# TensorE in program order, attention and M in tiles of two banks, weights converted by bits with seven blocks in flight, batch 0's second product by rows of w_out

## The chip, the cores and the metric

The kernel runs on one core of a Trainium2 chip. The metric is the device time of one execution in microseconds (us), the median of several runs. The engines are named as in the profile: PE is TensorE (PEld its weight loads), DVE is VectorE, ACT is ScalarE, POOL is GpSimd, SP is SyncE. SBUF is the memory on the core that all engines work in, PSUM the accumulators that PE writes; a bank of PSUM holds 512 fp32 values on each of 128 partitions, and there are eight.

## The reference

Per batch b (8 of them) and head h (8), x is 512 x 64 and state 32 x 64. Tokens read the states, states read the tokens, and the rows of both go through a feed-forward block with an ELU between its two products.

```python
scores  = x @ state.T / sqrt(64)          # 512 x 32
xread   = softmax(scores,  -1) @ state    # 512 x 64
scores2 = state @ x.T / sqrt(64)          # 32 x 512, the same numbers transposed
sread   = softmax(scores2, -1) @ x        # 32 x 64
rows    = concat([xread, sread])          # per batch 544 rows, heads side by side: 512 wide
h   = rows @ w_in                         # 4352 x 512 @ 512 x 2048
g   = where(h > 0, h, exp(min(h, 0)) - 1)
out = g @ w_out                           # 4352 x 2048 @ 2048 x 512
```

x and state are fp32, w_in and w_out arrive as 64-bit floats, and the output is fp32.

## The kernel before

**Setup.** The states are loaded with 32 small DMAs, half of them issued by SP and half by POOL, and turned by PE into kT (line 114). x of a batch, 1 MB, is loaded in four DMAs, two issued by SP and two by POOL (line 93); batches 0 and 1 at once, batch b+2 behind batch b+1's attention.

**Weights** (load_weights, lines 117 to 153). Both matrices come in 32 blocks of 128 x 512 64-bit values, 512 KB each: 16 of w_in (c is one of four groups of 512 columns, n one of four groups of 128 rows), 16 of w_out (fo is a group of 128 rows). A block is loaded into a "raw" tile (three tiles, which also held the states) by SP, and seven DVE steps over 128 x 512 elements make fp32 from the two 32-bit words of each value: exponent out, limited, moved, sign put in (lines 126 to 139), mantissa words joined and scaled (144 to 151). Every step that reads words of the raw tile reads every second word.

**Attention of a batch** (attention, lines 266 to 276), in steps: four times turn_x (four transposes on PE into one bank, a copy by ACT, line 168), scores (by_state, line 177: eight products of 64 x 32 weights, on parts of the array), two softmaxes (heads' halves g = 0, 1; lines 196 to 225) on DVE, ACT and POOL, one along the free dimension for the states (result a_s) and one in 32 x 32 blocks for the tokens (result t), turn_tokens (DVE transpose, aT), turn_state (four transposes of a_s on PE, copy by ACT to aT_s), state_read (16 products, line 246, result into xT_state for all batches), and the load of a later x.

**M.** xread @ w_in is not formed by way of xread. make_m (line 264) multiplies kT with 512 columns of w_in, by by_state in the same way as the scores, to M of 2 x 128 x 512; then h = aT @ M (ffn1, line 293) takes two products of 128 x 512 for each of the 16 groups fo of hidden columns.

**Feed-forward.** elu (lines 282 to 285): exp on ACT, min on DVE, then (e - 1) max h on DVE into g[fo]. ffn2 (line 318) sums 16 products over fo for each of four chunks c of 128 tokens, one PSUM bank (o_ps) for each; ACT or DVE copies it out (line 325), SP stores two chunks together (line 353). After the eight batches the 256 state rows go through the same block (lines 306, 318, 368).

**PSUM.** Eight banks: three one-bank tiles for everything in attention and M (ps_a), three for h, two for o.

**Order.** The text is written in program order: batch 0's attention with a load of w_in between its steps, the rest of w_in, M for the first columns; then per batch 16 times ffn1, with M for the next columns behind fo = 1, 5 and 9, a block of w_out (batch 0 only) and a step of the next batch's attention; then four chunks of ffn2, with M for the next batch behind chunk 2. A planner, which runs when the kernel is built, fixes the order of instructions on each engine before the run. It takes what is written first when its inputs are ready by its own estimate of times, on PE as on the other engines. Each engine then works through its own list in order, and DMAs issued by one engine are issued in that engine's order.

Of the kernel before, what the change touches and what calls it, by code (L numbers as in the profile page):

```python
# [15 lines left out]
PSUM = bass.MemoryType.PSUM  # L16


@with_exitstack
def kernel(  # L20
# [11 lines left out]
    nc = tc.nc  # L32
# [23 lines left out]
    cpool = ctx.enter_context(tc.tile_pool(name="const", bufs=1))  # L56
    xpool = ctx.enter_context(tc.tile_pool(name="x", bufs=2))
    apool = ctx.enter_context(tc.tile_pool(name="attn", bufs=2))
    xtpool = ctx.enter_context(tc.tile_pool(name="xT", bufs=4))
    atpool = ctx.enter_context(tc.tile_pool(name="aT", bufs=4))  # L60
    atspool = ctx.enter_context(tc.tile_pool(name="aT_s", bufs=1))
    mpool = ctx.enter_context(tc.tile_pool(name="m", bufs=2))
    rawpool = ctx.enter_context(tc.tile_pool(name="raw", bufs=3))
    wpool = ctx.enter_context(tc.tile_pool(name="pow", bufs=2))
    small = ctx.enter_context(tc.tile_pool(name="small", bufs=4))
    gpool = ctx.enter_context(tc.tile_pool(name="g", bufs=FO + 1))
    epool = ctx.enter_context(tc.tile_pool(name="elu", bufs=4))
    opool = ctx.enter_context(tc.tile_pool(name="o", bufs=2))
    ps_a = ctx.enter_context(tc.tile_pool(name="ps_a", bufs=3, space=PSUM))
    ps_h = ctx.enter_context(tc.tile_pool(name="ps_h", bufs=3, space=PSUM))  # L70
    ps_o = ctx.enter_context(tc.tile_pool(name="ps_o", bufs=2, space=PSUM))

    def bank(shape, name):
        return ps_a.tile(shape, FP32, tag="a", name=name)

# [13 lines left out]
    def load_x(b):  # L89
        x_t[b] = xpool.tile([P, R, DM], FP32, name="x_sb")  # L90
        x_v = x[b].rearrange("h (p r) d -> p r h d", r=R)
        for r in range(R):
            (nc.sync, nc.gpsimd)[r % 2].dma_start(
                out=x_t[b][:, r].rearrange("p (h d) -> p h d", d=D), in_=x_v[:, r]
            )

    def setup():
        make_identity(nc, ident)
        s_v = state.rearrange("(q b) (m c) n d -> q m b n c d", q=2, c=2)
        raw = [rawpool.tile([P, NP, P], FP32, tag="raw", name="s_sb") for q in range(2)]  # L100
        for q in range(2):
            for m in range(NP):
                for b in range(B // 2):
                    (nc.sync, nc.gpsimd)[q].dma_start(  # L104
                        out=raw[q][b * NS : (b + 1) * NS, m].rearrange("p (c d) -> p c d", c=2),
                        in_=s_v[q, m, b],
                    )
        for b in range(2):
            load_x(b)
        for q in range(2):  # L110
            ps = bank([P, NP, P], "k_ps")
            for m in range(NP):
                nc.tensor.transpose(ps[:, m], raw[q][:, m], ident)
            nc.vector.tensor_copy(out=kT[:, :, q * P : (q + 1) * P], in_=ps)

    def load_weights(dst, src):


        raw = rawpool.tile([P, 512], moe_w_in.dtype, name="raw")
        k = src.shape[-1]  # L120
        nc.sync.dma_start(out=raw.rearrange("p (j k) -> p j k", k=k), in_=src)
        words = raw.bitcast(U32).rearrange("p (j k w) -> p j k w", k=k, w=2)
        lo, hi = words[:, :, :, 0], words[:, :, :, 1]
        power = wpool.tile([P, 512], U32, name="power").rearrange("p (j k) -> p j k", k=k)

        nc.vector.tensor_scalar(  # L126
            out=power, in0=hi, scalar1=20, scalar2=0x7FF,
            op0=ALU.logical_shift_right, op1=ALU.bitwise_and,
        )
        low = 1023 - 127  # L130
        nc.vector.tensor_scalar(  # L131
            out=power, in0=power, scalar1=float(low), scalar2=float(low + 255),
            op0=ALU.max, op1=ALU.min,
        )
        nc.vector.tensor_scalar(  # L135
            out=power, in0=power, scalar1=float(-low), scalar2=float(1 << 23),
            op0=ALU.add, op1=ALU.mult,
        )
        nc.vector.scalar_tensor_tensor(  # L139
            out=power, in0=hi, scalar=0x80000000, in1=power,  # L140
            op0=ALU.bitwise_and, op1=ALU.bitwise_or,
        )

        nc.vector.tensor_scalar(  # L144
            out=hi, in0=hi, scalar1=0xFFFFF, scalar2=0x100000,
            op0=ALU.bitwise_and, op1=ALU.bitwise_or,
        )
        nc.vector.scalar_tensor_tensor(  # L148
            out=dst, in0=lo, scalar=2.0**-32, in1=hi, op0=ALU.mult, op1=ALU.add
        )  # L150
        nc.vector.scalar_tensor_tensor(  # L151
            out=dst, in0=dst, scalar=2.0**-20, in1=power.bitcast(FP32),
            op0=ALU.mult, op1=ALU.mult,
        )
    def load_w_in(c, n):
        cols = slice(c * 512, (c + 1) * 512)
        load_weights(w_in[:, n : n + 1, cols], w_in_v[:, n : n + 1, cols])

    def load_w_out(fo):
        load_weights(w_out[:, fo : fo + 1], w_out_v[:, fo : fo + 1])  # L160

    def turn_x(b, m):

        ps = bank([P, R, P], "xT_ps")
        for r in range(R):
            nc.tensor.transpose(ps[:, r], x_t[b][:, r, m * P : (m + 1) * P], ident)  # L166
        st[b, m] = xtpool.tile([P, R * P], FP32, name="xT")
        nc.scalar.copy(out=st[b, m], in_=ps.rearrange("p r q -> p (r q)"))  # L168

    def by_state(b, name, rhs):  # L170


        ps = [bank([P, 512], name) for g in range(G)]
        for m in range(NP):
            for g in range(G):
                d = slice(g * D, (g + 1) * D)
                nc.tensor.matmul(  # L177
                    ps[g][m * NS : (m + 1) * NS],
# [8 lines left out]
    def scores(b):  # L187

        for g, ps in enumerate(by_state(b, "s_ps", [st[b, m] for m in range(NP)])):
            softmaxes(b, g, ps)  # L190
# [41 lines left out]
    def turn_state(b, g):  # L232
        ps = bank([P, R, P], "sT_ps")
        a = st[b, g, "a_s"].rearrange("p (r q) -> p r q", r=R)
        for r in range(R):
            nc.tensor.transpose(ps[:, r], a[:, r], ident)  # L236
        if g == 0:
            st[b, "aT_s"] = atspool.tile([P, R, G, P], FP32, name="aT_s")
        nc.scalar.copy(out=st[b, "aT_s"][:, :, g], in_=ps)  # L239

    def state_read(b):

        ps = bank([P, NP, G, NS], "sr_ps")
        for m in range(NP):
            for r in range(R):
                nc.tensor.matmul(  # L246
                    ps[:, m],
                    x_t[b][:, r, m * P : (m + 1) * P],
                    st[b, "aT_s"][:, r, :, m * NS : (m + 1) * NS],
# [9 lines left out]
    def make_m(b, c):  # L259
# [3 lines left out]
        for g, ps in enumerate(by_state(b, "m_ps", [w_in[:, m, cols] for m in range(NP)])):  # L263
            (nc.scalar.copy, nc.vector.tensor_copy)[g % 2](out=m_t[b, c][:, g], in_=ps)  # L264

    def attention(b):
        steps = []
        steps += [lambda m=m: turn_x(b, m) for m in range(NP)]
# [132 lines left out]
```

## Time and profile before

| | us |
|---|---|
| median of 3 runs | 920.93 (920.3 to 921.58) |
| the profiled execution, its own time | 921.35 |
| the profiled execution, span of its trace | 919.6 |
| granted clock, mean over the span | 0.965 |

Busy time of each engine, and what the DMAs moved: PE 860.6 us, DVE 359.6, ACT 156.5, POOL 58.1; 35.07 MB. The span starts with the first instruction of the kernel; the profiled execution's own time has 1.75 us around it. In rows of a timeline the columns are start, length (both us), engine, line, operation, output and inputs, partitions x elements, and the count; matmul rows carry the size of the weights too. In rows of a view of stages they are the stage, its length, and busy time with the number of instructions for each engine, then the granted clock as a share, the DMAs' share and their rate.

### The profile page before, as it was taken

The page shows a single profiled execution, that of the slowest core. Times are in us where ns is not written, and L with a number is a line of the kernel's source. Part 1 is how long each engine was busy: PE and PEld are TensorE (multiplying, and loading weights), DVE is VectorE, ACT ScalarE, POOL GpSimd, SP SyncE. Part 2 cuts the span into 40 slices and gives each one's busy share as a digit, 9 for nine tenths or more (in the row PEclk, how much of TensorE's full clock was granted, in tenths as well). Part 3 has the DMA queues.
Part 4 walks back from the last instruction along what each step waited for, and adds up shares of the span by engine and source line. Part 5 has one row for each costly group of instructions (what it writes and reads, how often), then busy time and mean ns, then how long its engine had stood idle before and what let it go on. Part 6 is the DMA issues. An engine that isn't in the chain of part 4 may idle for free.

```text
span 919.6 us, 7252 instructions
## 1 busy us (share of the span) xinstructions
PE 860.6 (94%) x2824; PEld 392.7 (43%) x2824; DVE 359.6 (39%) x755; ACT 156.5 (17%) x290; POOL 58.1 (6%) x70
## 2 busy tenths in 40 slices
PE   4185889999999999999999999999999999999997
PEld 2141243445444444445444544454444444444773
DVE  1979999616102720183007500570027102600220
ACT  1111222113001310141004200330023101300110
POOL 5100020001000200010001100010001000000000
PEclk9565989999999999999999999999999999999999
DMA  7354333002000010002000200000000000000000
GB/s 178 96 160 143 131 100 131 23 24 47 0 24 23 16 32 23 24 1 46 24 0 24 47 0 24 23 1 1 23 24 1 0 23 24 1 0 24 23 1 23
DMA packets 27043, 35.07 MB, mean 38 GB/s; under 512 B 19329, under 2 KB 19585, under 8 KB 27009
## 3 DMA queue, kind: packets, MB, share of 16 engines
q1 hardware_dynamic: 25216, 30.15, 10.5%
q0 software_dynamic: 1792, 4.46, 2.1%
q8 instruction: 22, 0.36, 0.2%
q14 instruction: 13, 0.10, 0.0%
HBM read 25.69 MB, written 8.91 MB: 38 GB/s over the span
## 4 chain that ended last, share of the span: by engine, by line
PE 84%; DVE 9%; DMA 3%; ACT 1%; SPq 1%; issue 0%; POOL 0%; DVEq 0%; ACTq 0%; POOLq 0%
PE o_ps L318 50%; PE h_ps L293 22%; PE m_ps L177 4%; PE h_ps L306 3%; DMA raw<-in_moe_w_in_dram 3%; PE sr_ps L246 3%; PE xT_ps L166 1%; DVE power L139 1%; DVE w_in L148 1%; DVE power L131 1%; DVE power L126 1%; DVE g_sb L285 1%; SPq L104 1%; PE sT_ps L236 1%; DVE raw L144 1%; DVE power L135 1%
## 5 line engine op out<-in xcount | busy, mean ns | idle before, releaser
L318 PE MATMUL o_ps<-w_out,g_sb 128*128 128x512 f32 x1088 | 473.2, 593 | 1.7 <-DVE total L214 1.7
L318 PEld LDWEIGHTS o_ps<-w_out,g_sb 128*128 128x128 f32 x1088 | 205.5, 190 | 265.0 <-issue 257.2
L293 PE MATMUL h_ps<-aT,m_sb 128*128 128x512 f32 x512 | 244.4, 616 | 12.8 <-DVE g_sb L285 11.7
L293 PEld LDWEIGHTS h_ps<-aT,m_sb 128*128 128x128 f32 x512 | 94.3, 195 | 132.9 <-issue 89.6
L282 ACT ACTIVATE e_sb<-h_ps 128x512 f32<-128x512 f32 (+1 forms) x144 | 82.6, 573 | 329.1 <-PE h_ps L293 285.5
L325 DVE COPY o_sb<-o_ps 128x512 f32<-128x512 f32 x17 | 11.7, 691 | 324.0 <-PE o_ps L318 324.0
L283 DVE TENSOR_SCALAR e_sb<-e_sb 128x512 f32<-128x512 f32 (+1 forms) x144 | 63.9, 444 | 92.7 <-ACT e_sb L282 92.7
L285 DVE SCALAR_TENSOR_TENSOR g_sb<-e_sb,h_ps 128x512 f32<-128x512 f32 (+1 forms) x144 | 93.9, 652 | 12.0 <-PE o_ps L318 8.4
L325 ACT COPY o_sb<-o_ps 128x512 f32<-128x512 f32 x17 | 10.0, 586 | 304.8 <-PE o_ps L318 304.8
L177 PE MATMUL m_ps<-w_in,kT 64*32 64x512 f32 x512 | 54.4, 620 | 2.1 <-DVE w_in L151 1.0
L264 DVE COPY m_sb<-m_ps 128x512 f32<-128x512 f32 x32 | 21.8, 682 | 85.0 <-PE m_ps L177 84.9
L211 POOL TENSOR_TENSOR t_sb<-t_sb,top_t 128x512 f32<-128x512 f32 x16 | 17.4, 1088 | 575.7 <-DVE total L214 485.7
L246 PEld LDWEIGHTS sr_ps<-aT_s,x_sb 128*128 128x128 f32 x256 | 32.6, 209 | 7.7 <-ACT e_sb L282 5.0
L246 PE MATMUL sr_ps<-aT_s,x_sb 128*128 128x64 f32 x256 | 33.7, 295 | 0.7 <-ACT aT_s L239 0.7
L236 PE MATMUL sT_ps<-ident,a_s 128*128 128x128 f32 x64 | 11.3, 306 | 20.7 <-DVE a_s L218 19.9
L166 PE MATMUL xT_ps<-ident,x_sb 128*128 128x128 f32 x128 | 23.8, 315 | 4.6 <-ACT xT L168 2.4
L306 PE MATMUL h_ps<-xT_state,w_in 128*128 128x256 f32 x128 | 27.8, 379 | 0.0
L166 PEld LDWEIGHTS xT_ps<-ident,x_sb 128*128 128x128 f32 x128 | 17.5, 160 | 23.2 <-issue 10.0
L306 PEld LDWEIGHTS h_ps<-xT_state,w_in 128*128 128x128 f32 x128 | 24.3, 190 | 3.7 <-issue 0.5
L168 ACT COPY xT<-xT_ps 128x512 f32<-128x512 f32 x32 | 18.5, 586 | 33.8 <-PE xT_ps L166 33.8
L177 PEld LDWEIGHTS m_ps<-w_in,kT 64*32 64x32 f32 x512 | 8.2, 107 | 37.0 <-issue 23.6
L264 ACT COPY m_sb<-m_ps 128x512 f32<-128x512 f32 x32 | 18.7, 583 | 27.6 <-PE m_ps L177 27.6
(41 smaller groups left out, 310.2 us busy)
## 6 DMA issues: line engine op xcount, KB each, us to landing
raw<-in_moe_w_in_dram SPq DMA_DIRECT2D x16, 512.0 KB, 4.5
raw<-in_moe_w_out_dram SPq DMA_DIRECT2D x16, 512.0 KB, 3.4
out_dram<-o_sb SPq DMA_DIRECT2D x16, 512.0 KB, 2.6
x_sb<-in_x_dram SPq DMA_DIRECT2D x16, 256.0 KB, 4.1
x_sb<-in_x_dram POOLq DMA_DIRECT2D x16, 256.0 KB, 5.6
out_dram<-o_sb SPq DMA_DIRECT2D x8, 64.0 KB, 1.7
s_sb<-in_state_dram SPq DMA_DIRECT2D x16, 16.0 KB, 1.8
s_sb<-in_state_dram POOLq DMA_DIRECT2D x16, 16.0 KB, 2.0
```

What stands on the lines that cost most here:

```text
L166: nc.tensor.transpose(ps[:, r], x_t[b][:, r, m * P : (m + 1) * P], ident)
L177: nc.tensor.matmul(ps[g][m * NS : (m + 1) * NS], kT[d, m, b * NS : (b + 1) * NS], rhs[m][d], start=True, stop=True, tile_position=(g * D, ...
L236: nc.tensor.transpose(ps[:, r], a[:, r], ident)
L246: nc.tensor.matmul(ps[:, m], x_t[b][:, r, m * P : (m + 1) * P], st[b, "aT_s"][:, r, :, m * NS : (m + 1) * NS], start=(r == 0), stop=(r == ...
L264: (nc.scalar.copy, nc.vector.tensor_copy)[g % 2](out=m_t[b, c][:, g], in_=ps)
L282: nc.scalar.activation(out=e, in_=ps, func=AF.Exp)
L283: nc.vector.tensor_scalar(out=e, in0=e, scalar1=1.0, scalar2=None, op0=ALU.min)
L285: nc.vector.scalar_tensor_tensor(out=g[fo], in0=e, scalar=-1.0, in1=ps, op0=ALU.add, op1=ALU.max)
L293: nc.tensor.matmul(ps, m_t[b, fo // 4][:, k, fo % 4 * P : (fo % 4 + 1) * P], st[b, k, "aT"], start=(k == 0), stop=(k == G - 1),)
L306: nc.tensor.matmul(ps, w_in[:, co, fo * P : (fo + 1) * P], xT_state[:, co], start=(co == 0), stop=(co == NP - 1),)
L318: nc.tensor.matmul(ps, g[fo][:, c * P : (c + 1) * P], w_out[:, fo], start=(fo == 0), stop=(fo == FO - 1),)
L325: (nc.scalar.copy, nc.vector.tensor_copy)[c % 2](out=o_sb[:, c % 2], in_=ps)
```

## The change

The change has five parts.

1. **Order on PE.** Every matmul and transpose is handed to the planner with the demand to keep program order among them. The other engines' lists are planned as before.
2. **Tiles of two banks.** ps_a becomes a single tile of two banks instead of three of one; ps_o gets three banks. turn_x takes eight transposes at a time, by_state and turn_state fill both banks of the tile, and turn_state is one step for both halves. aT_s is laid out by halves first.
3. **Place of attention.** The next batch's attention is no longer spread over ffn1; its steps are called inside ffn2, one after every four products: turn_x, turn_x, scores, nothing, nothing, turn_state with turn_tokens, state_read, the load of x. M of the next batch is formed inside chunk 3.
4. **Weights.** A block is converted by three ACT steps and four DVE steps in place of seven DVE steps. The low three bits that the fp32 mantissa needs come from the low word by ACT (scaled, rounded by adding 2^23, taken off again); the high word goes as a 32-bit float through ACT's Abs, is limited by DVE, shifted by three as bits, gets sign and top exponent bit, and the low part is added. There are seven raw tiles instead of three and no tile for the power.
5. **Start.** States come in 16 DMAs, issued by SP and ACT; batch 0's x by SP and ACT, every other x by SP alone. Only w_in's first columns are asked for ahead of M and the rest of batch 0's attention; a block is asked for and converted behind each ffn1 of batch 0, x of batch 1 behind fo = 2, and M of the next columns comes behind fo = 3, 7 and 11. The blocks of w_out that are left are asked for and converted ahead of ffn2 in the text. Batch 0's ffn2 takes chunks 0, 1 and 2 together, for each fo, then chunk 3.

```diff
-    ps_a = ctx.enter_context(tc.tile_pool(name="ps_a", bufs=3, space=PSUM))
-    ps_h = ctx.enter_context(tc.tile_pool(name="ps_h", bufs=3, space=PSUM))
-    ps_o = ctx.enter_context(tc.tile_pool(name="ps_o", bufs=2, space=PSUM))
+    rawpool = pool("raw", 7)
+    ps_a = pool("ps_a", 1, space=PSUM)
+    ps_h = pool("ps_h", 3, space=PSUM)
+    ps_o = pool("ps_o", 3, space=PSUM)
...
+    def matmul(*args, **kw):
+        tc.keep_in_program_order(nc.tensor.matmul(*args, **kw))
+
+    def transpose(out, in_):
+        tc.keep_in_program_order(nc.tensor.transpose(out, in_, ident))
...
+    def convert(dst, raw):
+        words = raw.bitcast(U32).rearrange("p (j w) -> p j w", w=2)
+        lo, hi = words[:, :, 0], words[:, :, 1]
+        nc.scalar.activation(
+            out=lo.bitcast(FP32), in_=lo, func=AF.Copy, scale=2.0**-29, bias=2.0**23
+        )
+        nc.scalar.activation(out=lo, in_=lo.bitcast(FP32), func=AF.Copy, bias=-(2.0**23))
+        nc.scalar.activation(out=dst, in_=hi.bitcast(FP32), func=AF.Abs)
+        nc.vector.tensor_scalar(
+            out=dst, in0=dst, scalar1=as_float(896 << 20),
+            scalar2=as_float((1151 << 20) - 1), op0=ALU.max, op1=ALU.min,
+        )
+        bits = dst.bitcast(U32)
+        nc.vector.tensor_scalar(
+            out=bits, in0=bits, scalar1=3, scalar2=0x3FFFFFF8,
+            op0=ALU.logical_shift_left, op1=ALU.bitwise_and,
+        )
+        nc.vector.scalar_tensor_tensor(
+            out=bits, in0=hi, scalar=0xC0000000, in1=bits,
+            op0=ALU.bitwise_and, op1=ALU.bitwise_or,
+        )
+        nc.vector.tensor_tensor(out=bits, in0=bits, in1=lo, op=ALU.add)
...
+    def ffn2(g, chunks, o_sb, hooks, every):
+        ps = [ps_o.tile([P, DM], FP32, tag="o", name="o_ps") for c in chunks]
+        done = 0
         for fo in range(FO):
+            for c, o_ps in zip(chunks, ps):
+                matmul(o_ps, g[fo][:, c * P : (c + 1) * P], w_out[:, fo],
+                       start=(fo == 0), stop=(fo == FO - 1))
+                done += 1
+                if hooks and done % every == 0:
+                    hooks.pop(0)()
...
+    def attention(b):
+        nop = lambda: None
+        steps = [lambda: turn_x(b, 0), lambda: turn_x(b, 1), lambda: scores(b), nop, nop]
+        steps += [lambda: (turn_state(b), [turn_tokens(b, g) for g in range(G)])]
+        steps += [lambda: state_read(b)]
+        return steps
+
+    make_identity(nc, ident)
+    raw_states = load_states()
+    load_x(0, [nc.sync, nc.scalar])
+    todo = [load_w_in(0, n) for n in range(NP)]
+    turn_states(raw_states)
+    steps = attention(0)
+    for f in steps[:3]:
         f()
     for f in todo:
         f()
+    todo = [load_w_in(1, n) for n in range(NP - 1)]
     make_m(0, 0)
+    for f in steps[3:]:
+        f()
+    for f in todo:
+        f()
+    rest = [lambda c=c, n=n: load_w_in(c, n) for c in range(1, FC) for n in range(NP)][NP - 1 :]
+    rest += [lambda fo=fo: load_w_out(fo) for fo in range(FO)]
+
+    def more(k):
+        for f in rest[:k]:
+            f()()
+        del rest[:k]
+
     for b in range(B):
         g = {}
         for fo in range(FO):
             ffn1(g, b, fo)
+            if b == 0:
+                more(1)
+            if fo == 2 and b == 0:
+                load_x(1, [nc.sync])
-            if fo % 4 == 1 and fo // 4 + 1 < FC:
+            if fo % 4 == (3 if b == 0 else 1) and fo // 4 + 1 < FC:
                 make_m(b, fo // 4 + 1)
+        if b == 0:
+            more(len(rest))
+        nxt = b + 1 < B
+        hooks = attention(b + 1) if nxt else []
+        if b + 2 < B:
+            hooks += [lambda: load_x(b + 2, [nc.sync])]
...
+        for chunks in [[0, 1, 2], [3]] if b == 0 else [[0], [1], [2], [3]]:
+            if nxt and chunks == [3]:
+                hooks += [lambda: make_m(b + 1, 0)]
+            ffn2(g, chunks, o_sb, hooks, 4)
```

223 lines of the change are left out of this document (93 added, 130 removed).

## The prediction

> **What bounds the kernel now.** First the page: the span, the busy shares, and the slices.
>
> ```profile
> span 919.6 us, 7252 instructions
> ...
> PE 860.6 (94%) x2824; PEld 392.7 (43%) x2824; DVE 359.6 (39%) x755; ACT 156.5 (17%) x290; POOL 58.1 (6%) x70
> ...
> PE   4185889999999999999999999999999999999997
> ...
> DVE  1979999616102720183007500570027102600220
> ...
> PEclk9565989999999999999999999999999999999999
> ```
>
> One slice is 23 us. From slice 9 on PE is full at full clock, so only fewer or better packed matmul microseconds help there; before that PE has holes and DVE stands at 9. So there are two kernels in one, and the view of stages gives each its own numbers (columns: length, then busy us and instructions of PE, PEld, DVE, ACT, POOL; clock; DMA share; GB/s).
>
> ```profile
> 60.00:80.00 20.00, 15.80 (x50) 5.12 (x48) 19.78 (x44) 4.13 (x7) 0.00 (x0) 0.66 0.54 164
> 80.00:100.00 20.00, 11.20 (x32) 3.14 (x24) 19.60 (x44) 1.78 (x3) 0.00 (x0) 0.74 0.41 134
> 100.00:120.00 20.00, 14.57 (x39) 6.08 (x39) 18.86 (x44) 5.09 (x10) 3.58 (x3) 0.93 0.31 105
> 120.00:140.00 20.00, 20.00 (x82) 10.03 (x82) 19.86 (x45) 3.56 (x6) 2.97 (x3) 0.90 0.48 132
> 140.00:160.00 20.00, 19.74 (x72) 7.45 (x70) 19.91 (x45) 4.26 (x8) 0.00 (x0) 1.00 0.41 133
> 288.54:385.55 97.01, 96.92 (x329) 43.10 (x328) 30.57 (x62) 18.30 (x34) 5.93 (x6) 1.00 0.08 22
> 773.61:804.72 31.11, 31.11 (x113) 12.45 (x112) 18.95 (x34) 10.71 (x18) 0.00 (x0) 1.00 0.04 17
> 804.72:859.66 54.94, 54.94 (x130) 24.33 (x129) 2.07 (x4) 1.77 (x3) 0.00 (x0) 1.00 0.02 10
> 859.66:887.29 27.63, 27.63 (x130) 24.32 (x129) 11.41 (x31) 5.76 (x15) 0.00 (x0) 1.00 0.05 20
> 887.29:919.60 32.31, 27.62 (x65) 11.96 (x63) 1.41 (x3) 0.97 (x2) 0.00 (x0) 1.00 0.07 16
> ```
>
> From 60 to 160 us DVE is busy 98.0 of 100 us and ACT 18.8: the weights' conversion bounds the start. A middle batch takes 97.01 us. The last batch, which prepares no successor, takes 31.11 + 54.94 = 86.05, the state rows and the end 27.63 + 32.31 = 59.94. Six middle batches (1 to 6) make 582.1, so batch 1 begins in effect at 919.6 - 582.1 - 86.05 - 59.94 = **191.5 us**. The forecast is a new start, six new periods, and the end as it is.
>
> **The change part by part: the middle batches.** The number of matmuls does not change, only their order. (A product in fp32 stands in the trace as two MATMULs, a transpose as one.) PE's timeline of one batch:
>
> ```profile
> 290.25 0.60 PE L166 MATMUL xT_ps<-ident,x_sb 128*128 128x128 f32 x4
> 290.69 1.88 PE L293 MATMUL h_ps<-aT,m_sb 128*128 128x512 f32 x4
> ...
> 300.14 1.09 PE L177 MATMUL s_ps<-xT,kT 64*32 64x512 f32 x16
> ...
> 303.07 2.22 PE L177 MATMUL m_ps<-w_in,kT 64*32 64x512 f32 x16
> ...
> 311.51 1.04 PE L177 MATMUL m_ps<-w_in,kT 64*32 64x512 f32 x2
> ...
> 314.41 1.08 PE L177 MATMUL m_ps<-w_in,kT 64*32 64x512 f32 x14
> 315.42 3.79 PE L246 MATMUL sr_ps<-aT_s,x_sb 128*128 128x64 f32 x32
> ```
>
> An M normally takes 1.09; here one takes 2.22 and one is torn into 1.04 + 1.08. With both banks in one tile and a fixed order neither can happen: 1.1 + 1.0 = 2.1 us back. Built up from below: 128 matmuls of the second product are 54.94, so one is 0.429. The last batch's 31.11 holds 64 of them (27.5) and three M, hence 1.21 per M with its two switches of shape. Added to 86.05: a fourth M 1.21, the scores (same shape) 1.21, state read 3.8, 24 transposes at (290.69 - 290.25)/4 = 0.11, 2.6. Sum **94.9**, which is 97.01 less the same 2.1. Six times: 569.4.
>
> The move of attention out of the first product into the second takes DVE's softmax away from the ELU and puts it where DVE has 2.07 us of 54.94 busy: nothing on the path. The new waits there: one two-bank tile serves all of attention, so each step queues PE, with all matmuls behind it, until the copies of the step before are done. Steps are 4 products = 8 matmuls = 3.43 us apart; two ACT copies of about 0.6 each fit. Turning the state's weights comes three steps, 10.3 us, after the scores.
>
> ```profile
> 397.15 1.09 PE L177 MATMUL s_ps<-xT,kT 64*32 64x512 f32 x16
> ...
> 398.95 0.68 DVE L196 TENSOR_REDUCE top<-s_ps 128x1 f32<-128x512 f32 x1
> ...
> 406.08 1.06 DVE L218 TENSOR_SCALAR a_s<-a_s,total 128x512 f32<-128x512 f32 x1
> ```
>
> From the scores' start to the last a_s it is 10.0 us even with ELU work in between (about 2 us of it), so 8 alone: no wait, and 0 to 2 us a batch if it is not so. Three o_ps banks in place of two, and the other layout of aT_s: nothing, since PE is busy 54.94 of 54.94 us in the last batch's second product with two.
>
> **The start: conversion.** DVE's timeline while it is full; the distance of two starts is the true price, shorter than the duration:
>
> ```profile
> 76.18 0.68 DVE L148 SCALAR_TENSOR_TENSOR w_in<-raw 128x512 f32<-128x512 uint32 x1
> 76.78 0.68 DVE L139 SCALAR_TENSOR_TENSOR power<-raw,power 128x512 uint32<-128x512 uint32 x1
> 77.38 0.68 DVE L151 SCALAR_TENSOR_TENSOR w_in<-w_in,power 128x512 f32<-128x512 f32 x1
> 77.98 0.42 DVE L144 TENSOR_SCALAR raw<-raw 128x512 uint32<-128x512 uint32 x1
> 78.32 0.42 DVE L126 TENSOR_SCALAR power<-raw 128x512 uint32<-128x512 uint32 x1
> ...
> 85.10 0.42 DVE L126 TENSOR_SCALAR power<-raw 128x512 uint32<-128x512 uint32 x1
> ...
> 87.31 0.42 DVE L283 TENSOR_SCALAR e_sb<-e_sb 128x512 f32<-128x512 f32 x1
> ```
> ```profile
> 75.95 0.60 ACT L282 ACTIVATE e_sb<-h_ps 128x512 f32<-128x512 f32 x1 [4.47 <-PE h_ps L293]
> ```
>
> One-input steps cost 0.34, two-input steps 0.60. Before: 4 x 0.34 + 3 x 0.60 = 3.16 a block, 101 us for 32. After: two of each, 1.88, **60.2** for 32. The integer add of two tensors is in no row; it reads two inputs, so I take 0.60, with 0.34 and twice 0.60 as ends (-8 and +19 us). Three ACT steps join; Abs and the strided Copy are in no row either. The nearest:
>
> ```profile
> 18.36 1.56 ACT L168 COPY xT<-xT_ps 128x512 f32<-128x512 f32 x3 [16.34 <-PE xT_ps L166]
> ```
>
> That is 0.52 a step, 1.6 a block, 50 us for 32, beside some 23 us of ACT's other work of the start: 73, below DVE, and so hidden; at 0.8 a step ACT would be level with DVE.
>
> The last two fences also show how DVE's order is made. The first e_sb stood ready at 76.6, but its second step ran at 87.31, after a conversion that is written earlier: what is written first goes first, if its input is there. In the new text all conversions stand ahead of batch 1's softmax. So DVE does, in that order: batch 0's attention, 8.9 (a middle batch's 30.57 less 18.95, 2.07 and about 0.7 for an M copy), conversions 60.2, 16 ELU at 0.34 + 0.60, 15.0, four M copies 2.4: **86.5 us**. It begins when the first block is there:
>
> ```profile
> 0.74 7.44 SPq L104 DMA_DIRECT2D s_sb<-in_state_dram  x16
> 8.22 3.06 SPq L93 DMA_DIRECT2D x_sb<-in_x_dram  x4
> ...
> 12.00:14.00 2.00, 0.77 (x4) 0.36 (x2) 0.00 (x0) 0.00 (x0) 1.90 (x3) 1.00 1.30 236
> ...
> 20.00:22.00 2.00, 2.00 (x17) 0.40 (x16) 1.09 (x3) 0.58 (x1) 0.00 (x0) 1.00 1.02 293
> ```
>
> (From batch 2 on, x goes on SP alone: four issues at 3.06/4 = 0.77, POOL's share moved there, behind two output issues a batch and needed a batch later: nothing.) Eight state issues on SP (7.44/16 = 0.465 each) and two of x end at 6 us, ACT's ten beside them while ACT has no other work; 1 MB of x at 236 GB/s lands near 10.5, the first block at 293 GB/s near 12.3, ACT's three steps make it 14. Blocks then come every 1.8 us with seven tiles in flight, faster than DVE takes them (2.7 us, ELU and all). At 95% occupancy (98 above, less some idling in an order fixed beforehand) the conversions end at 14 + 86.5/0.95 = **105**.
>
> PE meanwhile is in program order: M, state turn, state read, first product. DVE has the attention and four blocks done at 14 + 8.9 + 7.5 = 30; the state read ran cold before,
>
> ```profile
> 44.99 7.09 PE L246 MATMUL sr_ps<-aT_s,x_sb 128*128 128x64 f32 x32 [0.68 <-ACT aT_s L239]
> ```
>
> so the first product starts near 38. Its last pair can run when the 13th ELU frees a bank; ahead of that ELU DVE has 8.9, 19 blocks (35.7), 13 ELU (12.2) and the M copies (2.4): 14 + 59.2/0.95 = 76, so the product ends near 78. (In batch 0 an M now comes directly ahead of its first use, so PE waits for its copies, 0.6 to 1.3 us three times; DVE is later anyway.) Batch 0's second product by rows with attention of batch 1 inside is 54.94 + 1.21 + 1.21 + 3.8 + 2.6 = 63.8 of PE work; unbroken it would end at 142. Its weights keep ahead: a row costs PE 2.6, DVE 1.88. But its sixth step, turning the state's weights, is due after 24 products (20.6), 16 transposes (1.8) and the scores (1.2), at 102, while the softmax begins only at 105 and takes 6 (the 8 above less PE's part): 111. PE waits some 9 us, and has then 40 products (34.3), 0.9, 3.8 and 1.21 left: **batch 1 begins at 151**. That wait is what takes the place of the old one.
>
> By the Trainium skill (TensorE: Matmul & The Clock Gate, Part 1) a wait of over about 3.4 us halves PE's clock until it has been busy as long; that would add an estimated 1.7 us here. The trace agrees in kind: in the second slice, with PE a tenth busy, the clock stands at 5.
>
> Sum: 151 + 569.4 + 86.05 + 59.94 = 866 of span. The profiled run took 921.35 for 919.6, 1.75 more (the median, 920.93, is 0.4 less): **868 us**.
>
> **The rivals.** (1) Batch 1's softmax slips into gaps of the conversions and PE never waits: start 142, 859 us. For it: ACT and the DMAs may leave gaps; against: the e_sb row. (2) The middle batches keep 97.0, since a step waits about 2 us for the single tile: 868 + 12.8 = 881. For it: the fixed order leaves PE nothing to put in; against: 3.43 us between steps. (3) DVE's order, made beforehand, meets a colder PE and idles 10 to 20 us: 878 to 888. For it: the rows from 60 to 120 us show clocks of 0.66 to 0.93; against: DVE at 98%. (4) Slower: Abs needs another activation table than Copy and Exp, so each block loads tables twice.
>
> ```profile
> 0.74 1.28 ACT L168 ACT_TABLE_LOAD   x1 [0.74 <-PEq L385]
> ```
>
> Then a block costs ACT 1.6 + 2 x 1.28 = 4.2, the conversions end at 12 + 23 + 134 = 169, batch 1 begins at 169 + 46 = 215, 932 us; it decides from 3.8 us a block. Against: Exp and Copy share one load here. The Trainium skill (ScalarE: Activation LUTs, Table sets) says Abs is in every set; no run here shows it yet.
>
> **How the numbers follow.** Forecast with its bounds 0.52, (1) 0.17, (2) 0.10, (3) 0.18, (4) 0.03. The range 852 to 888 holds the first four but for their edges: the add at 0.34 would give 860, at twice 0.60 887. Faster 0.96, same 0.01, slower 0.03; what a measurement can tell from no change is about 0.2%, 2 us.
>
> **What would show it.** A period of 95 between batches; DVE nearly full from 14 to 105 with four steps a block; PE idle near 100 to 111 ahead of the sT_ps transposes; one table load. A batch period of 97, or DVE with holes before 100, would break the sum.

## The result, and the profile after

The changed kernel takes 883.62 us (four runs, 882.49 to 884.65) against 921.14 (four runs, 920.30 to 921.58) beside it: a ratio of 0.9593, 95% interval 0.9576 to 0.9611, faster by 37.5 us. The forecast was 868, the range 852 to 888. The profiled execution took 884.56 us for a span of 882.8. Its page, in the lines that answer to those of before:

```profile
span 882.8 us, 7236 instructions
...
PE 838.0 (95%) x2824; PEld 391.5 (44%) x2824; DVE 323.8 (37%) x658; ACT 214.0 (24%) x386; POOL 35.8 (4%) x38
...
PE   3487979999999999999999999999999999999997
...
DVE  2869980263105340444026301632053403500220
PEclk9999989999999999999999999999999999999999
```

DVE's nines end in the fifth slice of 22 us, where before they went on into the seventh. But the second slice has an 8 and the third a 6 on DVE: the engine that bounds the start has holes early in it. The view of stages puts numbers to this (columns as before: length, busy us of PE, PEld, DVE, ACT, POOL, clock, DMA share, GB/s).

```profile
14.00:121.10 107.10, 81.44 (x273) 36.38 (x272) 89.99 (x191) 73.96 (x132) 4.78 (x4) 0.95 0.53 166
20.00:48.70 28.70, 15.39 (x65) 9.03 (x57) 21.38 (x47) 20.32 (x38) 4.78 (x4) 1.00 0.54 149
97.60:121.30 23.70, 23.70 (x81) 10.68 (x79) 23.70 (x52) 14.04 (x25) 0.00 (x0) 1.00 0.34 111
168.90:263.60 94.70, 94.70 (x330) 43.04 (x329) 31.34 (x62) 18.99 (x34) 4.33 (x4) 1.00 0.09 23
```

DVE did 90 us of work by 121.1, when the last conversion ended; 105 was forecast. From 20 to 48.7 it was idle for 7.3 us. Its timeline names the two largest holes, and shows the prices of the new steps as distances of starts (a bracket holds the idle time before a row and what ended it):

```profile
16.77 0.43 DVE L157 TENSOR_SCALAR w_in<-w_in 128x512 f32<-128x512 f32 x1 [5.00 <-ACT w_in L156]
...
48.94 0.59 DVE L281 COPY xT_state<-sr_ps 64x128 f32<-64x128 f32 x2 [5.30 <-PE sr_ps L86]
...
118.62 0.68 DVE L171 CUSTOM_DVE_ANT_0 w_out<-raw,w_out 128x1024 uint16<-128x1024 uint16 x1
119.22 0.68 DVE L167 SCALAR_TENSOR_TENSOR w_out<-raw,w_out 128x512 uint32<-128x512 uint32 x1
119.82 0.68 DVE L221 TENSOR_REDUCE top<-s_ps 128x1 f32<-128x512 f32 x1
120.42 0.68 DVE L171 CUSTOM_DVE_ANT_0 w_out<-raw,w_out 128x1024 uint16<-128x1024 uint16 x1
```

The integer add is there as CUSTOM_DVE_ANT_0 and costs 0.60 (118.62 to 119.22). The row at 119.82 is batch 1's softmax, among the last conversions as foreseen. And at 48.94 DVE had waited 5.30 us ahead of its copy of the state read, with conversions standing behind it in its list. PE's timeline shows why that read was late, and what followed:

```profile
38.68 1.97 PE L89 MATMUL sT_ps<-ident,a_s 128*128 128x128 f32 x8 [1.41 <-DVE m_sb L291]
41.81 7.09 PE L86 MATMUL sr_ps<-aT_s,x_sb 128*128 128x64 f32 x32 [1.16 <-ACT aT_s L265]
48.70 9.05 PE L86 MATMUL h_ps<-aT,m_sb 128*128 128x512 f32 x16
57.67 1.09 PE L86 MATMUL m_ps<-w_in,kT 64*32 64x512 f32 x16
61.12 1.12 PE L86 MATMUL h_ps<-aT,m_sb 128*128 128x512 f32 x2 [2.36 <-ACT m_sb L291]
...
97.61 3.60 PE L86 MATMUL o_ps<-w_out,g_sb 128*128 128x512 f32 x8
...
126.02 2.37 PE L89 MATMUL sT_ps<-ident,a_s 128*128 128x128 f32 x8 [4.68 <-ACT a_s L229]
128.18 5.07 PE L86 MATMUL o_ps<-w_out,g_sb 128*128 128x512 f32 x8
...
168.78 3.60 PE L86 MATMUL h_ps<-aT,m_sb 128*128 128x512 f32 x8
...
263.47 3.60 PE L86 MATMUL h_ps<-aT,m_sb 128*128 128x512 f32 x8
```

In program order M, the turning of the state and the state read stand ahead of the first product, so that product began at 48.7 (forecast 38) and ended at 97.6 (78). The forecast had M's four blocks at 30 and behind that little but the read of 7.09. They came at 35.3, and M's last products, their copies and the turning of the state took 6.5 us more before the read. Inside the product PE waits three times for M's copies, 2.9 to 3.7 us each (the first in two pieces, 2.36 and 0.54), where 0.6 to 1.3 were reckoned. The wait ahead of the state's transposes (sT_ps) is there, 4.68 us. Batch 1 begins at 168.8 (forecast 151), and the next period is 263.47 - 168.78 = 94.69 (94.9). Five more periods and the two unchanged ends give 168.8 + 6 x 94.69 + 86.05 + 59.94 = 882.9, the span. So the whole miss lies ahead of batch 1 (17.8 us; the periods gave 1.3 back), and the gain of 36.8 us of span is 6 x 2.32 = 13.9 from the periods and 191.5 - 168.8 = 22.7 from the start.

### The profile page after: what moved, and what is told of

Read it like the earlier page. It is cut to its first block, busy times and chain, and to the rows that moved or that the text cites. A ratio compares the mean times of both kernels' runs of the same rounds, so it can differ in the third digit from the quotient of the medians.

```text
span 882.8 us, 7236 instructions
## 1 busy us (share of the span) xinstructions
PE 838.0 (95%) x2824; PEld 391.5 (44%) x2824; DVE 323.8 (37%) x658; ACT 214.0 (24%) x386; POOL 35.8 (4%) x38
## 4 chain that ended last, share of the span: by engine, by line
PE 89%; DVE 6%; DMA 2%; ACT 2%; issue 1%; POOL 0%; SPq 0%; ACTq 0%
PE o_ps L86 51%; PE h_ps L86 28%; PE sr_ps L86 4%; PE m_ps L86 3%; PE xT_ps L89 1%; DMA raw<-in_moe_w_in_dram 1%; DVE w_out L167 1%; PE sT_ps L89 1%; PE s_ps L86 1%; DVE w_out L171 1%; DVE w_out L157 1%; DVE g_sb L300 0%; DVE w_out L163 0%; DVE w_in L167 0%; DMA x_sb<-in_x_dram 0%
## 5 line engine op out<-in xcount | busy, mean ns | idle before, releaser
L86 PE MATMUL o_ps<-w_out,g_sb 128*128 128x512 f32 x1088 | 478.6, 595 | 0.0
L86 PE MATMUL h_ps<-aT,m_sb 128*128 128x512 f32 x512 | 235.3, 613 | 9.7 <-ACT m_sb L291 6.4
L86 PEld LDWEIGHTS h_ps<-aT,m_sb 128*128 128x128 f32 x512 | 97.6, 195 | 146.0 <-issue 105.0
L298 DVE TENSOR_SCALAR e_sb<-e_sb 128x512 f32<-128x512 f32 (+1 forms) x144 | 59.3, 412 | 104.2 <-ACT e_sb L297 104.0
L347 DVE COPY o_sb<-o_ps 128x512 f32<-128x512 f32 x17 | 11.7, 691 | 175.4 <-PE o_ps L86 175.4
L86 PE MATMUL m_ps<-w_in,kT 64*32 64x512 f32 x512 | 39.5, 615 | 10.7 <-ACT a_s L229 7.4
L236 POOL TENSOR_TENSOR t_sb<-t_sb,top_t 128x512 f32<-128x512 f32 x16 | 16.9, 1059 | 645.0 <-DVE top_t L235 518.1
L221 DVE TENSOR_REDUCE top<-s_ps 128x1 f32<-128x512 f32 x16 | 11.0, 685 | 68.2 <-PE s_ps L86 68.2
L150 ACT ACTIVATE raw<-raw 128x512 f32<-128x512 uint32 x32 | 21.8, 680 | 12.9 <-DMA raw<-in_moe_w_in_dram 9.2
L86 PEld LDWEIGHTS m_ps<-w_in,kT 64*32 64x32 f32 x512 | 6.2, 105 | 39.4 <-issue 23.5
L281 DVE COPY xT_state<-sr_ps 64x128 f32<-64x128 f32 x16 | 4.6, 289 | 51.0 <-PE sr_ps L86 50.9
```

The source lines that it names most:

```text
L86: tc.keep_in_program_order(nc.tensor.matmul(*args, **kw))
L150: nc.scalar.activation(out=lo.bitcast(FP32), in_=lo, func=AF.Copy, scale=2.0**-29, bias=2.0**23)
L221: nc.vector.reduce_max(top, ps, axis=AX_X)
L236: nc.gpsimd.tensor_tensor(out=t, in0=t, in1=bc(top_t, NS), op=ALU.subtract)
L298: nc.vector.tensor_scalar(out=e, in0=e, scalar1=1.0, scalar2=None, op0=ALU.min)
L347: (nc.scalar.copy, nc.vector.tensor_copy)[c % 2](out=o_sb[c // 2][:, c % 2], in_=o_ps)
```

## The experiments

Two questions: what made the start 18 us longer than forecast, and which part of the change paid for what. In all that follows "conversions end" is the end of DVE's last step of a weight's conversion, "batch 1 begins" the first h_ps row of batch 1 (for the kernel before, whose planner had mixed the batches, the 191.5 of the prediction's subtraction); DVE's idle time is the sum of its gaps from the first conversion's step to the last one's. For the changed kernel these are 121.1, 168.8 and 14.3 us; for the kernel before the idle time was 8.7.

**Is it where M stands in batch 0?**

```diff
-            if fo % 4 == (3 if b == 0 else 1) and fo // 4 + 1 < FC:
+            if fo % 4 == 1 and fo // 4 + 1 < FC:
```

> Batch 0's M comes behind fo = 1, 5, 9 as in all other batches, two products ahead of its use. Theory A (the first product of batch 0 is long because PE waits for M's copies directly ahead of their use, 3 x about 3.2 us, and then runs at half clock for some us): the three gaps shrink to under 1 us each, the first product takes 49 - 10 to 15 us, batch 1 begins 8 to 13 us earlier than at 169. Rival B (DVE's conversions set the end of the first product, the gaps only use up time that DVE needs anyway): the gaps move elsewhere (waits for ELU or for w_in blocks), the first product stays within 3 us of 49, batch 1 begins within 3 us of 169. Middle batches 94.7 in both.

883.90 us, batch 1 at 168.8: nothing, as rival B had it. PE's timeline of this run, M's rows and the state's transposes:

```profile
65.08 1.05 PE L86 MATMUL m_ps<-w_in,kT 64*32 64x512 f32 x4 [1.56 <-DVE w_in L171]
68.22 1.05 PE L86 MATMUL m_ps<-w_in,kT 64*32 64x512 f32 x4 [2.09 <-DVE w_in L171]
...
82.20 1.05 PE L86 MATMUL m_ps<-w_in,kT 64*32 64x512 f32 x4 [2.69 <-DVE w_in L171]
...
126.17 2.37 PE L89 MATMUL sT_ps<-ident,a_s 128*128 128x128 f32 x8 [7.18 <-ACT a_s L229]
```

The waits for M's copies became waits for the blocks of w_in that M reads, and whatever was won came back ahead of sT_ps, 7.18 in place of 4.68: DVE sets the end of the conversions, and PE waits for it at one place or another.

**Is it the place of the state read?** M moves behind it.

```diff
-    make_m(0, 0)
     for f in steps[3:]:
         f()
+    make_m(0, 0)
```

> Batch 0's first M stands behind the state read instead of ahead of it. Theory A (PE's fixed order lets the state's transposes and read wait for the last of four blocks of w_in, 35.4 us, though their own input was there at 30): the first product begins 4 to 7 us earlier than at 48.7 and batch 1 begins earlier by as much or somewhat less. Rival B (DVE bound): the first product begins earlier, but waits inside, batch 1 begins within 2 us of 169.

878.33 us, as theory A had it; the conversions end at 115.5, DVE's idle time is 8.9, batch 1 begins at 162.9. PE's timeline:

```profile
32.89 7.09 PE L86 MATMUL sr_ps<-aT_s,x_sb 128*128 128x64 f32 x32 [1.16 <-ACT aT_s L265]
...
43.45 8.66 PE L86 MATMUL h_ps<-aT,m_sb 128*128 128x512 f32 x16 [0.73 <-ACT m_sb L291]
```

The read is 9 us earlier and as cold as before. DVE still waits 3.88 us for it (5.30 before), but no longer 1.71 for M's copy, and less for ELU's exp: it idles 5.4 us less, and the conversions end and batch 1 begins 5.6 and 5.9 us earlier. What DVE idles early is paid one for one at the end.

**Is it the cold clock of the read?** The same with nine products of the identity and x put ahead of the state's transposes, whose result is not read.

```diff
+    warm = ps_o.tile([P, DM], FP32, tag="o", name="o_ps")
+    for i in range(9):
+        matmul(warm, ident, x_t[0][:, 0], start=True, stop=True)
```

> As e2_m_after_state, with nine idle products ahead of the state's transposes that only keep PE busy (their result is not read). Theory D (the cold clock makes the state read take 7.1 us in place of 3.7 and DVE, whose list has the read's copy ahead of conversions, idles 3.9 us): the read takes 3.7 us, DVE's idle stretch of 3.9 us falls under 1, the first product begins 3 to 5 us earlier than e2's 43.5, batch 1 begins 2 to 5 us earlier than e2's 162.9. Rival (DVE idles for M or for ELU instead): the read is warm, but batch 1 begins within 1 us of e2's.

877.41 us (876.10 and 878.72): one of its two runs is no faster than the run without. In the profiled, faster one the read was only half warmed:

```profile
31.86 5.42 PE L86 MATMUL sr_ps<-aT_s,x_sb 128*128 128x64 f32 x32 [1.16 <-ACT aT_s L265]
```

It took 5.42 us where a warm one takes 3.68 and a cold one 7.09. The granted clock was 0.93 from 31.9 to 34.0 and 0.50 from there to 37.3: it fell inside the read. DVE's wait for the read fell from 3.88 to 1.86, not under 1. Conversions ended at 112.9 and batch 1 began at 160.3, both 2.6 earlier than without, but 0.7 of that is a first conversion that began earlier (16.3 for 17.0). The direction fits; two runs 2.6 us apart don't settle the size.

**Is it the tile of two banks?** ps_a becomes two tiles of one bank, the order stays (and kT is copied in two halves).

```diff
-    ps_a = pool("ps_a", 1, space=PSUM)
+    ps_a = pool("ps_a", 2, space=PSUM)
...
-    def banks(shape, name):
+    def bank(shape, name):
         return ps_a.tile(shape, FP32, tag="a", name=name)
+
+    def banks(shape, name):
+        return [bank(shape, name) for j in range(2)]
```

> All tiles of two banks are taken as two tiles of one bank (same PSUM, same order). Theory A (a tile of two banks lets its two readers on ACT and DVE run only one after the other): DVE's copy of M no longer waits for ACT's, each M gap of batch 0 is 0.6 to 1.4 us shorter, the middle batches stay at 94.7 (cover there), batch 1 begins 2 to 5 us earlier. Rival B (the copies are serial for another reason, their shared target tile): nothing changes, within 1 us. In both the two-bank tile has no part in the period.

883.70 us, no different. DVE's waits, of the changed kernel and then of this run (us in total, times, the longest):

```profile
DVE m_sb L291 <- ACT m_sb L291: 116.7, 9, 18.2
```
```profile
DVE m_sb L293 <- PE m_ps L89: 112.0, 8, 17.6
```

With one tile DVE's copy of M's second half is released by ACT's copy of the first, though they read different banks; with two tiles it is released by PE. So that wait went, against rival B, but the time didn't, against theory A. In batch 0 PE waits for M's copies nearly as long as before (2.6 to 3.5 us each time), so their one-after-the-other is not what those waits are made of. In the middle batches PE has other matmuls to run meanwhile; the period is the same 94.69 (167.09 to 261.78). In its profiled execution batch 1 began 1.7 us earlier, which the times don't confirm.

**Is it the order on PE?** The planner gets it back.

```diff
-        tc.keep_in_program_order(nc.tensor.matmul(*args, **kw))
+        nc.tensor.matmul(*args, **kw)
...
-        tc.keep_in_program_order(nc.tensor.transpose(out, in_, ident))
+        nc.tensor.transpose(out, in_, ident)
```

> Matmuls and transposes are planned freely again; all else is as in the changed kernel. Theory A (the order on PE gives the 2.3 us a batch): the period goes back to 96 to 97, +10 to +14 us in all, and the start changes by what the planner fills into PE's waits. Rival B (the two-bank tile and attention's place in the second product give it, not the order): the period stays at 94.7 within 0.3. On the start: if in-order PE costs it the 18 us by which it is late, batch 1 begins at 150 to 160; if not, at 165 to 172.

**867.85 us**, the fastest of all (ratio to before 0.9423, 0.9396 to 0.9450): the demand for program order costs 15.8 us. PE's timeline:

```profile
38.26 2.08 PE L86 MATMUL h_ps<-aT,m_sb 128*128 128x512 f32 x2 [0.69 <-ACT m_sb L291]
40.13 1.77 PE L89 MATMUL sT_ps<-ident,a_s 128*128 128x128 f32 x8
41.73 1.88 PE L86 MATMUL h_ps<-aT,m_sb 128*128 128x512 f32 x4
43.45 3.68 PE L86 MATMUL sr_ps<-aT_s,x_sb 128*128 128x64 f32 x32
...
99.60 1.09 PE L86 MATMUL s_ps<-xT,kT 64*32 64x512 f32 x16
100.62 19.15 PE L86 MATMUL o_ps<-w_out,g_sb 128*128 128x512 f32 x44
119.61 0.64 PE L89 MATMUL sT_ps<-ident,a_s 128*128 128x128 f32 x4
120.84 0.66 PE L89 MATMUL sT_ps<-ident,a_s 128*128 128x128 f32 x4 [0.60 <-DVE a_s L243]
...
151.88 3.60 PE L86 MATMUL h_ps<-aT,m_sb 128*128 128x512 f32 x8
```

Two things make the difference. Early, products of the first phase stand between the steps of the state read, which then runs warm, 3.68; the first product begins at 38.3, DVE idles 8.3 us in place of 14.3, and the conversions end at 114.7 (6.4 us earlier). Later, between the scores and the state's transposes there are 44 MATMULs of the second product where program order has 24: 20 x 0.429 = 8.6 us of work in the place of the wait, and the clock stays up. From the conversions' end to batch 1 it is 37.2 us here and 47.7 in program order. 6.4 + 10.5 = 16.9, the whole difference in batch 1's start.

**What is the conversion worth?** The seven old DVE steps, with the seven raw tiles and everything else of the change.

```diff
-        nc.scalar.activation(out=dst, in_=hi.bitcast(FP32), func=AF.Abs)
...
+        nc.vector.tensor_scalar(
+            out=power, in0=hi, scalar1=20, scalar2=0x7FF,
+            op0=ALU.logical_shift_right, op1=ALU.bitwise_and,
+        )
...
```

> Only the conversion is undone: seven DVE steps a block (3.16 us of DVE in place of 1.88, none of ACT), still seven raw tiles. Theory C (batch 1's begin is the end of the conversions, 121 us, plus 47 us): DVE has 32 x 1.28 = 41 us more, some of which falls into its 14 us of idling; conversions end at 150 to 162, batch 1 begins at 197 to 209, 912 to 924 us, and the whole gain against before shrinks to the period's 14 us or less. Rival (PE's waits set the start): batch 1 begins at 180 to 190.

915.16 us, as expected: the conversion is worth 31.5. PE's timeline has the rule of the start in one row; the conversions ended at 153.5:

```profile
157.59 2.37 PE L90 MATMUL sT_ps<-ident,a_s 128*128 128x128 f32 x8 [19.46 <-ACT a_s L236]
```

PE waits 19.46 us ahead of sT_ps, and batch 1 begins 46.7 after the conversions' end, as in every run with program order and all conversions ahead of batch 1's softmax (46.7 to 47.9).

**Rows of w_out against chunks.** `[[0, 1, 2], [3]] if b == 0 else [[0], [1], [2], [3]]` becomes `[[0], [1], [2], [3]]` for all batches.

> Batch 0's second product goes by chunks, as every other batch's. Theory C: the wait that ends last is that of the state's transposes for the softmax, which follows the conversions; by rows PE has 24 products done before it, by chunks the same 24, since the hooks count products; the conversions end at 121 as before, chunk 0 ends right behind them, 8 products later the transposes find their input ready: batch 1 begins at 167 to 171, no change beyond 2 us. Rival (rows let PE work while the conversions run, as the change intends): batch 1 begins 7 to 14 us later.

883.75 us and batch 1 at 168.0, as expected: no gain from the rows. PE's timeline by chunks:

```profile
103.32 1.12 PE L86 MATMUL o_ps<-w_out,g_sb 128*128 128x512 f32 x2 [0.56 <-DVE w_out L171]
...
118.31 1.12 PE L86 MATMUL o_ps<-w_out,g_sb 128*128 128x512 f32 x2 [1.08 <-DVE w_out L171]
...
127.95 1.04 PE L89 MATMUL sT_ps<-ident,a_s 128*128 128x128 f32 x8
```

By chunks the weights do come last: PE waits for their conversion nine times, 5.28 us in all, and has 18 MATMULs (7.7 us) less behind it when the conversions end. But then it finds the softmax done, with no wait ahead of the state's transposes and no cold clock behind it. By rows PE never waits for w_out, and pays 4.68 + 2.8 us there. The two prices are nearly equal here, so what the rows save, the softmax's place takes back.

**Conversions behind the softmax.** Only two blocks are called ahead of batch 0's second product, the others one per row inside it, so that batch 1's softmax stands among them in DVE's list.

```diff
-            more(len(rest))
+            more(2)
...
-            ffn2(g, chunks, o_sb, hooks, 4)
+            ffn2(g, chunks, o_sb, hooks, 4, lambda fo: more(1) if fo > 1 else None)
```

> The last seven blocks of w_out are converted in the text between the rows of batch 0's second product, so that batch 1's softmax comes ahead of four of them. Theory C: no wait of 4.7 us ahead of the state's transposes and no cold clock behind it (2.2 us); the conversions end later, which rows 12 to 15 bear; batch 1 begins at 160 to 163, 6 to 8 us earlier, 876 to 878 us. Rival (the rows then wait for their blocks): batch 1 begins at 167 or later.

876.39 us, as expected. PE's timeline:

```profile
120.24 0.60 PE L89 MATMUL sT_ps<-ident,a_s 128*128 128x128 f32 x4
```

The wait is gone although the conversions now end at 130.7; batch 1 begins at 160.6, 8.2 us earlier. So the wait did come from the softmax's place behind the conversions, as the prediction had it.

**Do the gains add?** Free order with late blocks; then also M behind the state read; then also M early. The edits are those shown above, put together.

> The changed kernel with PE planned freely (as e4_free_order) and the last seven blocks of w_out converted between the rows (as e7_late_blocks). Theory C (the wait ahead of the state's transposes was what both removed): the two gains, 16 and 7 us, do not add up; batch 1 begins at 149 to 153 where e4 has 151.9, 865 to 869 us. Rival (they act in different places): 860 us or less.

> As e12_free_rows, and the first M behind the state read. If DVE's idling at the start is what is left (8.3 us in e4), this takes 3 to 6 us of it and batch 1 begins at 145 to 149, 861 to 865 us; if PE's own holes between 38 and 82 us are (M's copies, ELU), the planner had already put products there and it stays at 150 to 153, 866 to 869 us.

> As e9_free_late, and batch 0's M behind fo = 1, 5, 9. Theory C: with PE planned freely M ahead of its use fills holes that in-order PE could not use (it gave nothing there): 2 to 5 us below e9. Rival (w_in's conversions come too late for it, as in e1): within 1 us of e9.

870.75, 871.24 and 869.74 us (four runs each): none is faster than free order alone. They lie 1.9 to 3.4 us above it, on another chip and with overlapping intervals (the ratios to before are 0.9453, 0.9458 and 0.9441, against 0.9396 to 0.9450). What was expected was missed in all three: the first two lie outside both ranges, and the third is 1.5 us below the second, between its theory and its rival, so M's place gives little here too. PE's timeline of the first:

```profile
99.92 10.57 PE L86 MATMUL o_ps<-w_out,g_sb 128*128 128x512 f32 x24
111.23 0.66 PE L89 MATMUL sT_ps<-ident,a_s 128*128 128x128 f32 x4 [0.74 <-ACT a_s L229]
114.19 1.11 PE L89 MATMUL sT_ps<-ident,a_s 128*128 128x128 f32 x4 [2.31 <-DVE a_s L243]
115.10 4.76 PE L86 MATMUL o_ps<-w_out,g_sb 128*128 128x512 f32 x8
```

Free order had filled the wait already. With the softmax moved ahead, the transposes again stand behind 24 MATMULs and not 44; but the softmax is then 3.05 us late (0.74 + 2.31, where free order alone waits 0.60), the second transposes take 1.11 in place of 0.66, and 8 MATMULs behind them 4.76 in place of 3.60. That makes 4.1 us; the scores began 0.7 earlier, and batch 1 begins 3.5 later (155.4 against 151.9). What estimate made the planner place them there was not looked at.

**The period.** The kernel before, in which attention, from batch 1 on, is called inside the second product; tiles, order and conversion stay as they were.

```diff
-            if todo:
+            if todo and b == 0:
                 todo.pop(0)()
...
-            ffn2(g, c, o_sb)
+            ffn2(g, c, o_sb, todo if b else ())
```

> The kernel before with one part of the change alone: from batch 1 on, the steps of the next batch's attention are called in the second product, one after every four products, in place of the first; matmuls planned freely, tiles of one bank, seven DVE steps. Theory E (the place of attention gives the shorter period, neither PE's order nor the two-bank tile): the period falls from 97.0 to 94.7 +- 0.4, the start stays within 4 us, 905 to 911 us. Rival (order and tile are needed so that M isn't torn): the period stays above 96, 916 to 922 us.

909.39 us (four runs, ratio 0.9878, 0.9864 to 0.9893), as expected. PE's timeline:

```profile
287.85 3.60 PE L293 MATMUL h_ps<-aT,m_sb 128*128 128x512 f32 x8
291.37 1.09 PE L177 MATMUL m_ps<-w_in,kT 64*32 64x512 f32 x16
...
382.54 3.60 PE L293 MATMUL h_ps<-aT,m_sb 128*128 128x512 f32 x8
```

The period is 382.54 - 287.85 = 94.69, and M takes 1.09, with three tiles of one bank and PE's order left to the planner. The place of attention alone gives the whole of the period's gain. Of the 13.9 us that six such periods save the time shows 11.7: batch 1 begins in effect at 193.2, 1.7 later than before.

In one view (us; the last column is the median):

| run | conversions end | batch 1 begins | time |
|---|---|---|---|
| before | 168.9 | 191.5 (by subtraction) | 921.14 |
| the change | 121.1 | 168.8 | 883.62 |
| M early | 121.2 | 168.8 | 883.90 |
| M behind the state read | 115.5 | 162.9 | 878.33 |
| the same, with idle products | 112.9 | 160.3 | 877.41 |
| tiles of one bank | 119.2 | 167.1 | 883.70 |
| by chunks | 120.1 | 168.0 | 883.75 |
| old conversion | 153.5 | 200.2 | 915.16 |
| blocks late | 130.7 | 160.6 | 876.39 |
| **order left to the planner** | 114.7 | 151.9 | **867.85** |
| the same, blocks late | 126.1 | 155.4 | 870.75 |
| the same, M behind the state read | 126.9 | 154.7 | 871.24 |
| the same, M early | 127.0 | 153.9 | 869.74 |
| before, attention moved | 168.6 | 193.2 (by subtraction) | 909.39 |

## Why the prediction was right in sign and range, and where it failed

- **The two regimes** were read rightly: the start and the six periods account for the span to 0.1 us, and the ends are as they were.
- **The periods, 94.9:** measured 94.69. The number, built up from below, was right, and rival 2 is out; the cause it was given is not needed for it. The text put it down to "both banks in one tile and a fixed order". Tiles of one bank keep 94.69, a free order keeps 94.68 (151.88 to 246.56), and the kernel before reaches 94.69 by moving attention alone. With attention elsewhere M is not torn. Whether order and tile would have done it too, with attention in its old place, no run shows.
- **The conversion's price:** the add at 0.60 was the right choice between its ends, and 1.88 a block on DVE held (3.75 for two, start to start). ACT's step was taken at 0.52 and is 0.565; it stays hidden. ACT's timeline in the start:

```profile
7.10 1.28 ACT L150 ACT_TABLE_LOAD   x1 [7.10 <-DMA s_sb<-in_state_dram]
14.01 0.65 ACT L150 ACTIVATE raw<-raw 128x512 f32<-128x512 uint32 x1 [5.63 <-DMA raw<-in_moe_w_in_dram]
...
58.81 0.67 ACT L150 ACTIVATE raw<-raw 128x512 f32<-128x512 uint32 x1
59.38 0.65 ACT L156 ACTIVATE w_in<-raw 128x512 f32<-128x512 f32 x1
59.94 0.66 ACT L153 ACTIVATE raw<-raw 128x512 uint32<-128x512 f32 x1
```

  ACT did 73.96 us in the start, where 73 was forecast. There is one table load and none between Abs (L156) and Copy: rival 4 is out, and this trace agrees with what the Trainium skill (ScalarE: Activation LUTs, Table sets) says of Abs.
- **The step that failed: "At 95% occupancy the conversions end at 105".** They ended at 121.1. The first conversion started on DVE at 16.8 and not 14 (+2.8; the first block came at 14.0, not 12.3, and ACT put copies of xT between its steps). DVE's work to the last conversion was 90.0 and not 86.5 (+3.5; 1.8 of it are three conversion steps between 28.2 and 34.1 that took 0.56, 1.19 and 1.53 in place of 0.42, 0.42 and 0.68, while POOL worked on the softmax; the cause was not tried). And it idled 14.3 us where 5% is 4.5 (+9.8). The 95% came from a stretch in which DVE had long been behind; the holes lie earlier, where DVE's list, made beforehand, waits for others: 5.3 us for the state read, 5.5 in pieces for ELU's exp, 1.7 for M's copy. That was rival 3, at its price (878 to 888), and in part with its reason, a colder PE: the read was taken from a cold row, 7.09, but PE's late arrival at it and its effect on DVE's list, the 5.30 us hole, were not worked out. A warm read shortens the hole (2.60 in free order). M behind the state read shortens it only to 3.88, but with the other waits it saves 5.4 us of idling, and the time follows by 5.3.
- **The wait for the state's weights:** right in place and cause (late blocks remove it, the old conversion lengthens it to 19.46), so rival 1 is out. It measured 4.68 and not 9, because PE was late too. From the conversions' end to batch 1 the forecast had 46, and it is 47.7. The cold clock behind the wait is in that (granted 0.50 from 126.0 to 128.2 and 0.70 from there to 133.1): the transposes took 2.37 in place of 1.04, and 8 MATMULs 5.07 in place of 3.60, together 2.8 us, where 1.7 was estimated from the rule of the Trainium skill (TensorE: Matmul & The Clock Gate, Part 1).
- **Program order was costed at nothing but this wait**, and at the waits for M that DVE was to cover. Measured against the planner's order, these included, it is 15.8 us of time. That the run without it lands on the forecast's 868 is a coincidence: the forecast reached 151 with earlier conversions and a wait, that run with later conversions and hardly a wait (0.60).
- **By rows of w_out:** the text argued that the weights keep ahead. By rows they do, by chunks they don't (5.28 us of waits); but the rows' gain is lost again in the wait for the softmax, so batch 0's rows bring nothing as the change has them.

So of the gain (36.8 us of span), the periods (place of attention) give about 14 and the start 22.7. Undone singly, the conversion takes back 31.5 us and the order on PE gives 15.8; rows and two-bank tiles show no effect on the time. At batch 1's start, 31.4 from the conversion less 16.9 for the order leaves 14.5 of 22.7. The rest, about 8, is not accounted for: it may lie in the loads, the raw tiles and the place of batch 0's steps, or in how the two depend on each other; these weren't tried apart.

## What to carry to other kernels

A start bounded by one engine is forecast from the waits in that engine's list, one by one, and not from a share of busy time taken where it is already saturated: in these runs each microsecond idled early was paid at the end. A fixed order on the matmul engine needs a look at every step that waits for another engine, because nothing fills the wait and the clock falls as well; the planner's own order, with attention moved to where the other engines are free, was the fastest version here. And a number that comes out right can still stand on a wrong cause: the period was predicted to 0.2 us, and another part of the change gives it alone.

## What was not expected of the hardware

- The state read, 32 MATMULs of 64 columns with a weight load each, ran 7.09 us without a gap at half speed (3.68 warm), and the 16 full-width MATMULs behind it took 9.05 in place of 7.13, so the first 1.92/0.429 = 4.5 of them were still cold, some 3.8 us. That it was the clock is inferred: the granted clock of this stretch stands at 1.00 in the profile, as it does from the first instruction on, but the same read at 45.0 of the kernel before took the same 7.09 at a granted 0.50, and the warm one at 133.1 took 3.68 at 1.00. By the Trainium skill (TensorE: Matmul & The Clock Gate, Part 1) about 3.4 us of sustained work warms the clock; here that holds for the wide products, while 7 us of narrow ones did not do it, and with idle products ahead the clock fell inside the read (0.93 to 0.50).
- Two engines that copy different banks of one two-bank tile went one after the other (DVE's copy waited for ACT's); with two tiles they did not. Whether the order comes from the planner's tracking of the tile or from the chip, no run separates.
- The 32-bit integer add ran as 128x1024 of uint16, at 0.60 the same price as a two-input step over 512 words.
